# Two pairs of PSUM banks for the attention's output, rows normalised one unit later, expert 0's first chunk in the scores' banks

## The chip, the core and the metric

One core of one Trainium2 chip. The engines are TensorE (PE, with its weight loads as PEld), VectorE (DVE), ScalarE (ACT), GpSimd (POOL) and SyncE (SP, which here only issues transfers). Each runs its own instructions in order; semaphores tie them together. [...] The metric is the time of one execution on the device in microseconds, median of several runs.

## What is computed

Sliding-window attention over 8 batches of 8 heads, 576 positions, head dimension 64, then a mixture of 8 experts with two chosen per token, all in fp32:

```python
scores = scale * q @ k.T                       # masked to 0 <= pos_q - pos_k < 64
attn = exp(scores - max); attn /= sum(attn) + 1e-9
x = (attn @ v) as rows [4608, 512]             # token rows, heads side by side
noisy = x @ w_gate + log1p(exp(x @ w_noise)) * noise
top2 of noisy, softmax over the two -> weights
out = sum over the two chosen e of weight * (relu(x @ w1[e]) @ w2[e])
```

## The kernel before

**Units.** The attention runs over 36 units `j`: block `i` of 64 positions (nine) times a pair of batches `bp` (four). One unit gives 128 token rows. A unit needs four loads (`qc`, `KW`, `vt`, 256 KB each; `vw`, 272 KB) and one store of its rows to the DRAM tensor `X` (256 KB), all issued by SP. Since the window is one block long, a unit reads the keys and values of its own block and of the one before.

**The loop** (L723 on) is software-pipelined; the order of the calls in its body is the order of every engine's queue. In iteration `j` stand, in order: loads for units `j+2` and `j+3`; `scores(j)` (L242, TensorE, two banks `ps_s`); `soft_b(j-1)` (exp on ScalarE), `soft_a(j)` (ScalarE copies the scores), `pv(j-2)` (L300, 64 matmuls into the two banks `ps_o`, one pair); `soft_max(j)` (VectorE, masked copy), `norm_a(j-2)` (L318, VectorE: reciprocal of the row sums, and `gm`, the logits' share of `ps_o` times the reciprocal), `soft_max2(j)` (VectorE maximum, GpSimd subtraction); `norm_b(j-2)` (L327, ScalarE: eight copies of 64 elements with a per-row scale, `ps_o` to the tile `x`); `store(j-3)`; `transp(j-1)` (L283, TensorE, bank `ps_t`); `logits(j+1)` (L216, TensorE, bank `ps_x`, 16 matmuls of `vt` with the gate weights, whose result `logits_copy` (L226) puts beside the values so that `pv` carries the logits along); `apply_mask(j-1)` (VectorE, `ps_t` to `pt`); `gate(j-2)` (L342, VectorE sums `gm` over the heads).

**The routing** of 6 to 9 units (`route`, L396) is a list of small steps on `[128, n, 8]`, mostly on VectorE, some on ScalarE, with one rank computation on TensorE in bank `ps_g`. `drain(rate(q))` puts 0 to 2 of them at five places of each iteration, by `RATE` (L43); `HOLD` (L42) makes it skip some calls ahead of the rank matmul. Its results are scattered as list entries to DRAM by GpSimd, two transfers a unit of the routing, issued by `drain_slots`. GpSimd then gathers expert 0's rows by such a list, which SP loads.

**Expert 0's first chunk** (384 rows) starts inside the loop: `turn(0, 0)` (L575) transposes three gathered tiles on TensorE into the single bank `ps_m` and splits them in two parts on ScalarE and VectorE; it is set into iterations 31 and 32 (`TURN`, L36). `ahead` (L702) then places 15 of 32 steps of `up(0, 0)` (three matmuls each, accumulated in `ps_m`, four steps a tile) into iterations 33 to 36. After the loop the attention's banks are given to the experts, which run 24 chunks with TensorE at the centre.

**Banks before:** `ps_g` (warm-up, ranks), `ps_x` (logits), `ps_m` (expert 0's start), `ps_s` two, `ps_t` one, `ps_o` two: eight. `load_rest` (L169) issues in iteration 3 eight transfers: the noise, a zeroed stretch of `X`, and the padding of the lists.

Of the kernel before, what the change touches and what calls it, by code (L numbers as in the profile page):

```python
# [34 lines left out]
W1G = 12  # L35
TURN = 31  # L36
AHEAD = 15
SLOTS = 5
WARM = 4

ZEROS = (15, 28, 37)
HOLD = 4  # L42
RATE = ((15, 6), (20, 8), (26, 6), (99, 8))  # L43

# [19 lines left out]
def tile_kernel(ctx, tc, qT, kT, vx, vT, wgx, noise, w1, w2, out):  # L64
# [103 lines left out]

    def load_rest():  # L169
        nc.sync.dma_start(noise_sb, noise)  # L170
        nc.sync.dma_start(X[0:DUMP, :], zero)
        o = LIST * 2
        for n in CHUNKS:
            w = n // 32 * 2
            nc.sync.dma_start(rows(L, o, [[w, 32], [LIST * 2, E - 1], [1, w]]),
                              pad_f[:, None, :w].to_broadcast([32, E - 1, w]))
            o += n * 2
        pad_t = pad_o.rearrange("k p c -> k (p c)")
        nc.sync.dma_start(rows(L, 0, [[256, CAP // 128], [1, 256]]), pad_t[:CAP // 128])
        nc.sync.dma_start(rows(L, CAP // 128 * 256, [[256, 1], [1, CAP % 128 * 2]]), pad_t[:1, :CAP % 128 * 2])  # L180
        nc.sync.dma_start(rows(L, CAP * 2, [[256, OVT], [LIST * 2, E], [1, 256]]),
                          pad_o.rearrange("k p c -> k (p c)")[:, None, :].to_broadcast([OVT, E, 256]))

# [29 lines left out]

    VG = ps.tile([128, 4, 128], F32, name="ps_x")

    def logits(j):  # L216
        p = VG[:, j % 4]
        x = VT.pop(j)
        for u in range(2):
            for g in range(2):  # L220
                for a in range(2):
                    q = u * 2 + g
                    nc.tensor.matmul(p[a * 64:a * 64 + 64, q * 32:q * 32 + 32], lhsT=x[:, q, a * 64:a * 64 + 64],
                                     rhs=wgx_sb[:, g * 2 + a, :], start=True, stop=True)

    def logits_copy(j):  # L226
        i, bp = divmod(j, NP)
        nc.scalar.activation(VW[bp][:, i % 2, 4, :, :, 0:16].rearrange("p u k e -> p (u k) e"),
                             VG[:, j % 4].rearrange("p (k e) -> p k e", e=16), AF.Copy)

# [65 lines left out]

    PO, RS, GM = {}, {}, {}


    def pv(j):  # L300
        i, bp = divmod(j, NP)
        o = aps.tile([128, 2, 512], F32, name="ps_o")
        PO[j] = o[:, :, 0:340].rearrange("p a (k d) -> p a k d", d=85)
# [14 lines left out]
    def norm_a(j):  # L318
        r = wk.tile([128, 2, 4], F32, name="r")
        RS[j] = r  # L320
        nc.vector.tensor_scalar(r, PO[j][:, :, :, 16], 1e-9, None, op0=OP.add)
        nc.vector.reciprocal(r, r)
        GM[j] = wk.tile([128, 8, 16], F32, name="gm")
        nc.vector.tensor_tensor(GM[j].rearrange("p (a k) e -> p a k e", a=2), PO[j][:, :, :, 68:84],  # L324
                                r[:, :, :, None].to_broadcast([128, 2, 4, 16]), op=OP.mult)

    def norm_b(j, a):  # L327
        if j not in XT:
            XT[j] = gw.tile([128, H, 64], F32, name="x", bufs=3)
        o, r = PO[j][:, a, :, 0:68].rearrange("p k (q d) -> p k q d", d=17), RS[j][:, a]  # L330
        for k in range(4):
            nc.scalar.activation(XT[j][:, a * 4 + k].rearrange("p (q d) -> p q d", d=16), o[:, k, :, 0:16], AF.Copy,  # L332
                                 scale=r[:, k:k + 1])

    def store(j):
        nc.sync.dma_start(X[DUMP + j * 128:DUMP + (j + 1) * 128, :], XT.pop(j).rearrange("p h d -> p (h d)"))

# [237 lines left out]
    def turn(e, c):  # L575
# [6 lines left out]
        def f(q, m):  # L582
# [5 lines left out]
            else:  # L588
                y = bank()[:, :KD * m].rearrange("p (k m) -> p k m", k=KD)
                for k in range(KD):  # L590
# [7 lines left out]
        return [lambda q=q, m=m, x=x: x(q, m) for q, m in tiles(c) for x in (f, g)]  # L598

    def bank():  # L600
        if "up" in BANKS:
            return BANKS["up"].tile([128, 512], F32, name="ps_u", bufs=3)
        return ps.tile([128, 512], F32, name="ps_m")

# [115 lines left out]

    logits(0)
    logits_copy(0)
    for j in range(NT + 2):  # L723
        if j == TURN:
            for q, f in enumerate(turn(0, 0)):
                aux.setdefault(j + q // 3, []).append(f)
        if 0 < j < NT - 3:
# [10 lines left out]
        if NT - 2 <= j:  # L738
# [24 lines left out]
        on(gate, j - 2)  # L763
        drain(rate(3))
# [4 lines left out]
    store(NT - 1)  # L769
    for q in range(max(aux), NT + 1, -1):  # L770
        for f in aux.get(q, ()):
            f()
# [56 lines left out]
    ov = ctx.enter_context(tc.tile_pool(name="ov", bufs=1))  # L829

    def overflow(e, k):
        a1 = ov.tile([128, KD, F], F32, name="a1")
# [5 lines left out]
        if e == 0:  # L838
# [53 lines left out]
def layout(inputs):  # L892
# [44 lines left out]
```

## Time and profile before

| | |
|---|---|
| median of 3 runs | 1097.46 us (1096.47 to 1099.86) |
| the profiled execution | 1103.63 us, of it the span 1101.9 us |
| TensorE busy | 1015.8 us (92%) |
| VectorE, ScalarE, GpSimd busy | 454.0, 384.4, 537.7 us |
| transferred | 133.45 MB |

The profile's page and its queries are views of one execution, whose times count from the start of its span. "Busy" is the union of an engine's instructions; a matmul's end is modelled, so starts are the surer numbers. [...] A bracket at a row's end is the idle time of that engine just before, and what ended it; "issue" means nothing that the profile shows.

### The profile page before, as it was taken

What the parts mean: (1) busy time and instruction counts of PE and PEld (TensorE: products, weight loads), DVE (VectorE), ACT (ScalarE), POOL (GpSimd) and SP (SyncE); (2) the same over time, 40 slices, a digit from 0 to 9 for tenths busy, and PEclk for the clock granted to TensorE, in tenths of its full rate; (3) what the DMA queues carried; (4) which work ended last, traced back from release to release, by engine and by line L of the source; (5) the groups of instructions that cost most, each with busy time, mean ns of one, the idle gap of its engine ahead of it and who ended that gap; (6) DMA issues with size and microseconds to landing.
All of it is one profiled execution on the core that took longest, in us unless ns stands there. A gap on an engine that the chain in (4) does not pass through costs nothing. (4 is left out here: it accounts for less than half of the span.)

```text
span 1101.9 us, 20457 instructions
## 1 busy us (share of the span) xinstructions
PE 1015.8 (92%) x8313; PEld 902.1 (82%) x8313; DVE 454.0 (41%) x979; ACT 384.4 (35%) x975; POOL 537.7 (49%) x612
## 2 busy tenths in 40 slices
PE   8677776889996999999999999999999999999994
PEld 8566665778795889988998899888989888988893
DVE  5588676553134233522452244224422533262220
ACT  3566454432133223422342234224322522252220
POOL 4346544566255555453555356524654465455411
PEclk9899887999998999999999999999999999999997
DMA  8989977469824422632263235324423452333122
GB/s 290 342 253 253 234 187 263 127 178 229 230 55 129 103 48 51 202 55 39 45 204 57 40 92 157 58 37 121 130 49 44 115 134 46 51 51 53 37 25 31
DMA packets 62681, 133.45 MB, mean 121 GB/s; under 512 B 16776, under 2 KB 17266, under 8 KB 60786
## 3 DMA queue, kind: packets, MB, share of 16 engines
q1 hardware_dynamic: 39986, 92.11, 26.6%
q0 software_dynamic: 22592, 39.95, 20.7%
q8 instruction: 67, 1.10, 0.4%
q14 instruction: 36, 0.29, 0.1%
HBM read 92.31 MB, written 39.70 MB: 120 GB/s over the span
## 5 line engine op out<-in xcount | busy, mean ns | idle before, releaser
L570 POOL DMA_INDIRECT xg<-xrows,ixs x266 | 259.0, 974 | 81.2 <-issue 75.1
L626 PE MATMUL ps_u<-xh,w1h 128*128 128x384 f32 (+1 forms) x752 | 261.0, 347 | 12.1 <-ACT xh L596 11.4
L627 PE MATMUL ps_u<-xl,w1h 128*128 128x384 f32 (+1 forms) x752 | 260.8, 347 | 0.0
L628 PE MATMUL ps_u<-xh,w1l 128*128 128x384 f32 (+1 forms) x752 | 260.5, 346 | 0.0
L641 POOL DMA_INDIRECT out_dram<-yo,lts x70 | 113.1, 1615 | 295.8 <-ACT yo L661 152.5
L656 PE MATMUL ps_d<-w2h,hh 128*128 128x512 f32 x576 | 225.4, 391 | 0.0
L657 PE MATMUL ps_d<-w2l,hh 128*128 128x512 f32 x576 | 225.1, 391 | 0.0
L658 PE MATMUL ps_d<-w2h,hl 128*128 128x512 f32 x576 | 225.0, 391 | 0.0
L633 DVE SCALAR_TENSOR_TENSOR hl<-ps_u,hh 128x384 fp32r<-128x384 f32 x188 | 104.7, 557 | 269.6 <-ACT hh L632 269.6
L632 ACT ACTIVATE hh<-ps_u 128x384 fp32r<-128x384 f32 x188 | 92.5, 492 | 239.3 <-PE ps_u L628 239.1
L626 PEld LDWEIGHTS ps_u<-xh,w1h 128*128 128x128 f32 x752 | 142.1, 189 | 17.9 <-ACT xh L596 12.3
L627 PEld LDWEIGHTS ps_u<-xl,w1h 128*128 128x128 f32 x752 | 142.0, 189 | 5.5 <-DVE xl L597 0.9
L628 PEld LDWEIGHTS ps_u<-xh,w1l 128*128 128x128 f32 x752 | 142.0, 189 | 3.8
L656 PEld LDWEIGHTS ps_d<-w2h,hh 128*128 128x128 f32 x576 | 108.5, 188 | 23.7 <-issue 1.8
L658 PEld LDWEIGHTS ps_d<-w2h,hl 128*128 128x128 f32 x576 | 108.5, 188 | 22.8
L657 PEld LDWEIGHTS ps_d<-w2l,hh 128*128 128x128 f32 x576 | 108.5, 188 | 21.9
L661 ACT ACTIVATE yo<-ps_d,lts 128x512 f32<-128x512 f32 x63 | 43.4, 690 | 195.7 <-PE ps_d L658 118.4
L597 DVE TENSOR_TENSOR xl<-xy,xh 128x512 fp32r<-128x512 f32 (+1 forms) x70 | 46.7, 667 | 147.5 <-ACT xh L596 147.5
L332 ACT ACTIVATE x<-ps_o,r 128x64 f32<-128x64 f32 x288 | 63.2, 330 | 70.4 <-DVE gm L324 22.5
L276 POOL TENSOR_TENSOR t<-t,mx 128x512 f32<-128x512 f32 x36 | 37.5, 1042 | 99.4 <-DVE mx L275 47.9
L311 PE MATMUL ps_o<-vw,pt 64*64 64x85 f32 x2176 | 56.1, 254 | 24.7 <-ACT x L332 18.5
L472 POOL DMA_INDIRECT slots<-val,posi x72 | 70.6, 980 | 15.0 <-issue 14.5
(146 smaller groups left out, 964.7 us busy)
## 6 DMA issues: line engine op xcount, KB each, us to landing
w2s<-in_w_dram SPq DMA_DIRECT2D x7, 2048.0 KB
w1s<-in_w_dram SPq DMA_DIRECT2D x7, 2048.0 KB
vw<-in_vx_dram SPq DMA_DIRECT2D x36, 272.0 KB
out_dram<-zero SPq DMA_DIRECT2D x37, 256.0 KB
qc<-in_qT_dram SPq DMA_DIRECT2D x36, 256.0 KB
KW<-in_kT_dram SPq DMA_DIRECT2D x36, 256.0 KB
vt<-in_vT_dram SPq DMA_DIRECT2D x36, 256.0 KB
xrows<-x SPq DMA_DIRECT2D x36, 256.0 KB
```

The lines of the kernel that those rows point to most:

```text
L332: nc.scalar.activation(XT[j][:, a * 4 + k].rearrange("p (q d) -> p q d", d=16), o[:, k, :, 0:16], AF.Copy, scale=r[:, k:k + 1])
L472: s = nc.gpsimd.indirect_dma_start(out=L, out_offset=bass.IndirectOffsetOnAxis(ap=posi[:, c2, q:q + 1], axis=0), in_=val[:, c2, q, :], in_ ...
L570: nc.gpsimd.indirect_dma_start(out=XG[e, c, t // 4][:, t % 4, :], out_offset=None, in_=XQ[:(DUMP + seen.get((e, c), NT) * 128) * 4], in_of ...
L626: nc.tensor.matmul(p[:, :n], lhsT=w1h[:, k, fs], rhs=xh[:, k, :n], start=(k == 0), stop=False)
L627: nc.tensor.matmul(p[:, :n], lhsT=w1h[:, k, fs], rhs=xl[:, k, :n], start=False, stop=False)
L628: nc.tensor.matmul(p[:, :n], lhsT=w1l[:, k, fs], rhs=xh[:, k, :n], start=False, stop=(k == KD - 1))
L632: nc.scalar.activation(h, p[:, :main], AF.Relu)
L633: nc.vector.scalar_tensor_tensor(l, p[:, :main], 0.0, h.bitcast(F32), op0=OP.max, op1=OP.subtract)
L641: nc.gpsimd.indirect_dma_start(out=out[:DUMP + seen.get((e, c), NT) * 128], out_offset=bass.IndirectOffsetOnAxis(ap=LT[e, c][:m, q, 0:1], ...
L656: nc.tensor.matmul(p, lhsT=hh[f][:, sl], rhs=w2h[:, f, :], start=(f == 0), stop=False)
L657: nc.tensor.matmul(p, lhsT=hh[f][:, sl], rhs=w2l[:, f, :], start=False, stop=False)
L658: nc.tensor.matmul(p, lhsT=hl[f][:, sl], rhs=w2h[:, f, :], start=False, stop=(f == KF - 1))
```

## The change

`ps_o` becomes two pairs of banks. `norm_a`, `norm_b`, `store` and `gate` run one iteration later, so the loop has one iteration more; `norm_a` comes first in the iteration, `store` among the loads. `gm` is gone: `norm_b` copies 80 columns a head, the logits among them, to a tile whose order is part, head, column; `X` and `w1` take that order of columns, `w1` on the host. The logits' accumulators move from `ps_x` to the warm-up's bank, two slots for four, and `logits(j)` runs in iteration `j`. The routing's steps are drained at other places, `HOLD` is 6, `RATE` shifts by an iteration. `load_rest`'s transfers are spread over iterations 3 to 7. `turn(0, 0)` begins in iteration 33 at two steps an iteration, in the bank `ps_t`; 16 steps of `up(0, 0)` are placed in iterations 36 to 38, in the two banks of `ps_s` in turn. `ps_x` and `ps_m` are gone; the overflow code, which runs only where an expert has more rows than its list, gets a pool of its own.

```diff
-TURN = 31
-AHEAD = 15
+TURN = 33
+AHEAD = 16
...
-HOLD = 4
-RATE = ((15, 6), (20, 8), (26, 6), (99, 8))
+HOLD = 6
+RATE = ((16, 6), (21, 8), (27, 6), (99, 8))
...
+    REST = [lambda: nc.sync.dma_start(noise_sb, noise), lambda: nc.sync.dma_start(X[0:DUMP, :], zero),
+            lambda: load_pads(0), lambda: load_pads(1), lambda: load_pads(2)]
...
-    VG = ps.tile([128, 4, 128], F32, name="ps_x")
+    VG = idle[:, 0:256].rearrange("p (n c) -> p n c", n=2)
...
-        o = aps.tile([128, 2, 512], F32, name="ps_o")
+        o = aps.tile([128, 2, 512], F32, name="ps_o", bufs=2)
...
         nc.vector.reciprocal(r, r)
-        GM[j] = wk.tile([128, 8, 16], F32, name="gm")
-        nc.vector.tensor_tensor(GM[j].rearrange("p (a k) e -> p a k e", a=2), PO[j][:, :, :, 68:84],
-                                r[:, :, :, None].to_broadcast([128, 2, 4, 16]), op=OP.mult)
...
-            XT[j] = gw.tile([128, H, 64], F32, name="x", bufs=3)
-        o, r = PO[j][:, a, :, 0:68].rearrange("p k (q d) -> p k q d", d=17), RS[j][:, a]
+            XT[j] = gw.tile([128, 5, H, 16], F32, name="x", bufs=3)
+        o, r = PO[j][:, a].rearrange("p k (q d) -> p k q d", d=17), RS[j][:, a]
         for k in range(4):
-            nc.scalar.activation(XT[j][:, a * 4 + k].rearrange("p (q d) -> p q d", d=16), o[:, k, :, 0:16], AF.Copy,
-                                 scale=r[:, k:k + 1])
+            nc.scalar.activation(XT[j][:, :, a * 4 + k], o[:, k, :, 0:16], AF.Copy, scale=r[:, k:k + 1])
...
-        nc.vector.tensor_reduce(LG[c][:, j - ROUTE[c]], GM.pop(j).rearrange("p k e -> p e k"), op=OP.add, axis=AX.X)
+        nc.vector.tensor_reduce(LG[c][:, j - ROUTE[c]], XT[j][:, 4].rearrange("p h e -> p e h"), op=OP.add, axis=AX.X)
...
+        if not pair:
+            p = aps.tile([128, 2, 4, 128], F32, name="ps_s").rearrange("p u g c -> p u (g c)")
+            pair.extend([p[:, 1], p[:, 0]])
+        return pair.pop()
...
+        return aps.tile([128, 4, 128], F32, name="ps_t").rearrange("p k c -> p (k c)")
...
-            if j >= TURN + 2 and len(taken) < AHEAD:
+            if j >= NT and len(taken) < AHEAD:
...
-    logits(0)
-    logits_copy(0)
-    for j in range(NT + 2):
+    for j in range(NT + 3):
         if j == TURN:
             for q, f in enumerate(turn(0, 0)):
-                aux.setdefault(j + q // 3, []).append(f)
+                aux.setdefault(j + q // 2, []).append(f)
...
-        if j == 3:
-            load_rest()
+        on(store, j - 4)
+        if 2 < j < 3 + len(REST):
+            REST[j - 3]()
...
+        on(norm_a, j - 3)
+        drain(rate(0))
         on(scores, j)
         on(soft_b, j - 1)
         on(soft_a, j)
-        drain(rate(0))
-        ahead(1)
+        ahead(2)
+        drain(rate(1))
         on(pv, j - 2)
-        drain(rate(1))
+        on(norm_b, j - 3, 0)
         on(soft_max, j)
-        on(norm_a, j - 2)
         on(soft_max2, j)
         drain_slots(1)
-        on(norm_b, j - 2, 0)
-        on(store, j - 3)
-        drain(rate(2))
         if j < NP:
             warm(WARM)
-        ahead(1)
         on(transp, j - 1)
-        on(norm_b, j - 2, 1)
-        on(logits, j + 1)
         ahead(2)
+        on(logits, j)
+        on(norm_b, j - 3, 1)
         on(apply_mask, j - 1)
-        on(logits_copy, j + 1)
-        on(gate, j - 2)
+        drain(rate(2))
+        on(logits_copy, j)
+        ahead(2)
+        on(gate, j - 3)
```

## Rows read from the trace of the kernel before

**Rows 1.** By stretch: us, busy (x count) per engine, PEclk, DMA share, GB/s.

```profile
7.60:24.00 16.40, 16.31 (x302) 14.67 (x304) 8.21 (x17) 4.95 (x19) 4.59 (x7) 1.00 1.01 351
24.00:221.00 197.00, 147.48 (x3847) 125.55 (x3847) 137.62 (x371) 109.70 (x413) 95.63 (x143) 0.90 0.80 235
...
330.00:1101.90 771.90, 745.40 (x3661) 669.20 (x3659) 266.83 (x482) 236.38 (x470) 374.44 (x337) 0.99 0.35 79
```

**Rows 2.** Waits of PE, 0 to 221 us: total us, times, longest us.

```profile
PE ps_o L311 <- ACT x L332: 18.5, 18, 1.4
PE ps_x L223 <- DMA vt<-in_vT_dram: 9.3, 3, 4.1
PE ps_s L252 <- issue: 5.5, 3, 2.5
PE ps_o L311 <- issue: 5.4, 6, 3.1
```

**Rows 3.** Timeline of PE: start us, length us; scores of units 0, 9, 18, 33; expert 0.

```profile
8.58 1.13 PE L254 MATMUL ps_s<-KW,qc 64*64 64x64 f32 x32
...
51.05 1.10 PE L252 MATMUL ps_s<-KW,qc 64*64 64x128 f32 x32
...
97.05 1.10 PE L252 MATMUL ps_s<-KW,qc 64*64 64x128 f32 x32
...
193.07 1.99 PE L252 MATMUL ps_s<-KW,qc 64*64 64x128 f32 x32
...
221.78 0.34 PE L626 MATMUL ps_u<-xh,w1h 128*128 128x384 f32 x1
```

**Rows 4.** Timeline of all engines inside one unit, 95 to 100 us.

```profile
95.12 0.22 DVE L423 TENSOR_TENSOR l<-l,noise_sb 128x56 f32<-128x56 f32 x1
...
96.27 0.72 DVE L270 COPY_PREDICATED t<-mprev,ps_s 128x512 f32<-128x512 uint32 x1
...
97.31 0.29 DVE L324 TENSOR_TENSOR gm<-ps_o,r 128x128 f32<-128x128 f32 x1
...
97.68 1.75 ACT L332 ACTIVATE x<-ps_o,r 128x64 f32<-128x64 f32 x8 [2.09 <-PE ps_x L223]
...
98.22 1.22 DVE L293 TENSOR_TENSOR pt<-ps_t,maskT 128x1024 f32<-128x1024 f32 x1
...
99.36 0.36 DVE L346 TENSOR_REDUCE lg<-gm 128x16 f32<-128x128 f32 x1
...
99.54 1.28 PE L311 MATMUL ps_o<-vw,pt 64*64 64x85 f32 x57 [1.39 <-ACT x L332]
```

**Rows 5.** Timeline of PE: three long waits of the attention.

```profile
35.12 1.07 PE L223 MATMUL ps_x<-wgx_sb,vt 128*64 128x32 f32 x16 [4.06 <-DMA vt<-in_vT_dram]
...
168.40 1.07 PE L223 MATMUL ps_x<-wgx_sb,vt 128*64 128x32 f32 x16 [3.45 <-DMA vt<-in_vT_dram]
...
182.64 1.12 PE L591 MATMUL ps_m<-ident,xg 128*128 128x128 f32 x4 [3.09 <-DVE xl L597]
```

**Rows 6.** By stretch, single units; columns as in rows 1.

```profile
118.00:126.90 8.90, 6.45 (x120) 5.69 (x119) 5.47 (x17) 4.02 (x16) 3.44 (x6) 0.62 0.81 200
46.00:51.00 5.00, 3.66 (x116) 3.15 (x116) 3.23 (x7) 3.53 (x13) 2.47 (x3) 1.00 1.05 386
61.90:67.10 5.20, 3.70 (x119) 3.11 (x119) 4.97 (x14) 3.53 (x13) 2.47 (x3) 1.00 0.84 257
97.00:103.20 6.20, 3.96 (x124) 3.29 (x121) 5.73 (x19) 3.20 (x13) 4.16 (x7) 1.00 0.97 248
```

**Rows 7.** Timeline of PE: the step after the one at 221.78.

```profile
222.31 0.33 PE L626 MATMUL ps_u<-xh,w1h 128*128 128x384 f32 x1
```

**Rows 8.** The page: instruction queue's packets, MB; the scatters' group, idle before them.

```profile
q8 instruction: 67, 1.10, 0.4%
...
L472 POOL DMA_INDIRECT slots<-val,posi x72 | 70.6, 980 | 15.0 <-issue 14.5
```

**Rows 9.** Waits of PE, 221 to 450 us.

```profile
PE ps_u L591 <- DMA xg<-xrows,lt: 2.4, 1, 2.4
```

More of the change, by code (lines that the diff above doesn't have):

```diff
@@ L167, in tile_kernel, with load_pads @@
     noise_sb = consts.tile([128, NT, E], F32)
[L169 to L177, printed above, removed]
-        pad_t = pad_o.rearrange("k p c -> k (p c)")
[L179 to L182, printed above, removed]
+    def load_pads(q):
+        if q == 0:
+            o = LIST * 2
+            for n in CHUNKS:
+                w = n // 32 * 2
+                nc.sync.dma_start(rows(L, o, [[w, 32], [LIST * 2, E - 1], [1, w]]),
+                                  pad_f[:, None, :w].to_broadcast([32, E - 1, w]))
+                o += n * 2
+            return
+        pad_t = pad_o.rearrange("k p c -> k (p c)")
+        if q == 1:
+            nc.sync.dma_start(rows(L, 0, [[256, CAP // 128], [1, 256]]), pad_t[:CAP // 128])
+            nc.sync.dma_start(rows(L, CAP // 128 * 256, [[256, 1], [1, CAP % 128 * 2]]), pad_t[:1, :CAP % 128 * 2])
+        else:
+            nc.sync.dma_start(rows(L, CAP * 2, [[256, OVT], [LIST * 2, E], [1, 256]]),
+                              pad_t[:, None, :].to_broadcast([OVT, E, 256]))
+    REST = [lambda: nc.sync.dma_start(noise_sb, noise), lambda: nc.sync.dma_start(X[0:DUMP, :], zero),
+            lambda: load_pads(0), lambda: load_pads(1), lambda: load_pads(2)]
     def zero_out(t):
@@ L211, in split_w2 @@
         return [lambda f=f: split(w2s[:, f], W2["h"][:, f], W2["l"][:, f]) for f in range(KF)]
-    VG = ps.tile([128, 4, 128], F32, name="ps_x")
+    VG = idle[:, 0:256].rearrange("p (n c) -> p n c", n=2)
     def logits(j):
-        p = VG[:, j % 4]
+        p = VG[:, j % 2]
         x = VT.pop(j)
@@ L228, in logits_copy @@
         nc.scalar.activation(VW[bp][:, i % 2, 4, :, :, 0:16].rearrange("p u k e -> p (u k) e"),
-                             VG[:, j % 4].rearrange("p (k e) -> p k e", e=16), AF.Copy)
+                             VG[:, j % 2].rearrange("p (k e) -> p k e", e=16), AF.Copy)
     ST, T, P, TP, PT, XT = {}, {}, {}, {}, {}, {}
@@ L295, in apply_mask @@
                                 op=OP.mult)
-    PO, RS, GM = {}, {}, {}
+    PO, RS = {}, {}
     def pv(j):
         i, bp = divmod(j, NP)
-        o = aps.tile([128, 2, 512], F32, name="ps_o")
+        o = aps.tile([128, 2, 512], F32, name="ps_o", bufs=2)
         PO[j] = o[:, :, 0:340].rearrange("p a (k d) -> p a k d", d=85)
@@ L322, in norm_a @@
         nc.vector.reciprocal(r, r)
-        GM[j] = wk.tile([128, 8, 16], F32, name="gm")
-        nc.vector.tensor_tensor(GM[j].rearrange("p (a k) e -> p a k e", a=2), PO[j][:, :, :, 68:84],
-                                r[:, :, :, None].to_broadcast([128, 2, 4, 16]), op=OP.mult)
     def norm_b(j, a):
         if j not in XT:
-            XT[j] = gw.tile([128, H, 64], F32, name="x", bufs=3)
-        o, r = PO[j][:, a, :, 0:68].rearrange("p k (q d) -> p k q d", d=17), RS[j][:, a]
+            XT[j] = gw.tile([128, 5, H, 16], F32, name="x", bufs=3)
+        o, r = PO[j][:, a].rearrange("p k (q d) -> p k q d", d=17), RS[j][:, a]
         for k in range(4):
-            nc.scalar.activation(XT[j][:, a * 4 + k].rearrange("p (q d) -> p q d", d=16), o[:, k, :, 0:16], AF.Copy,
-                                 scale=r[:, k:k + 1])
+            nc.scalar.activation(XT[j][:, :, a * 4 + k], o[:, k, :, 0:16], AF.Copy, scale=r[:, k:k + 1])
     def store(j):
-        nc.sync.dma_start(X[DUMP + j * 128:DUMP + (j + 1) * 128, :], XT.pop(j).rearrange("p h d -> p (h d)"))
+        nc.sync.dma_start(X[DUMP + j * 128:DUMP + (j + 1) * 128, :],
+                          XT.pop(j)[:, 0:4].rearrange("p q h d -> p (q h d)"))
     LG, PG = {}, {}
@@ L588, in f @@
             else:
-                y = bank()[:, :KD * m].rearrange("p (k m) -> p k m", k=KD)
+                y = turn_bank()[:, :KD * m].rearrange("p (k m) -> p k m", k=KD)
                 for k in range(KD):
@@ L598, in turn @@
         return [lambda q=q, m=m, x=x: x(q, m) for q, m in tiles(c) for x in (f, g)]
+    pair = []
     def bank():
@@ L602, in bank, with turn_bank @@
             return BANKS["up"].tile([128, 512], F32, name="ps_u", bufs=3)
-        return ps.tile([128, 512], F32, name="ps_m")
+        if not pair:
+            p = aps.tile([128, 2, 4, 128], F32, name="ps_s").rearrange("p u g c -> p u (g c)")
+            pair.extend([p[:, 1], p[:, 0]])
+        return pair.pop()
+    def turn_bank():
+        if "up" in BANKS:
+            return bank()
+        return aps.tile([128, 4, 128], F32, name="ps_t").rearrange("p k c -> p (k c)")
     EXB, BANKS = {}, {}
@@ L737, in tile_kernel @@
             load_w1(0, slice(k, k + 1))
-        if NT - 2 <= j:
+        if NT - 2 <= j < NT + 2:
             load_w2(0, slice((j - NT + 2) * 2, (j - NT + 3) * 2))
+        on(norm_a, j - 3)
+        drain(rate(0))
         on(scores, j)
@@ L769, in tile_kernel @@
     store(NT - 1)
-    for q in range(max(aux), NT + 1, -1):
+    for q in range(max(aux), NT + 2, -1):
         for f in aux.get(q, ()):
@@ L829, in tile_kernel @@
     ov = ctx.enter_context(tc.tile_pool(name="ov", bufs=1))
+    ops = ctx.enter_context(tc.tile_pool(name="ops", bufs=1, space=bass.MemoryType.PSUM))
     def overflow(e, k):
@@ L842, in overflow @@
                                          in_offset=bass.IndirectOffsetOnAxis(ap=lt[:, 0:1], axis=0))
-            xp = ps.tile([128, KD, 128], F32, name="ps_x")
+            xp = ops.tile([128, KD, 128], F32, name="ps_x")
             for d in range(KD):
@@ L865, in overflow @@
         for f in range(KF):
-            hp = ps.tile([128, 128], F32, name=("ps_m", "ps_x")[f % 2])
+            hp = ops.tile([128, 128], F32, name=("ps_m", "ps_x")[f % 2])
             for d in range(KD):
@@ L912, in layout @@
     noise = inputs["moe_noise"].reshape(NP, 2, NB, 64, E).transpose(1, 3, 2, 0, 4).reshape(128, NT, E)
-    w1 = inputs["moe_w1"].reshape(E, 4, KD, 32, F).transpose(0, 1, 3, 2, 4).reshape(E, 128, KD, F)
-    w1 = np.concatenate([inputs["moe_w1"][:1].reshape(1, KD, 128, F).transpose(0, 2, 1, 3), w1[1:]])
+    w1x = inputs["moe_w1"].reshape(E, H, 4, 16, F).transpose(0, 2, 1, 3, 4).reshape(E, DM, F)
+    w1 = w1x.reshape(E, 4, KD, 32, F).transpose(0, 1, 3, 2, 4).reshape(E, 128, KD, F)
+    w1 = np.concatenate([w1x[:1].reshape(1, KD, 128, F).transpose(0, 2, 1, 3), w1[1:]])
     w2 = inputs["moe_w2"].reshape(E, KF, 128, DM).transpose(0, 2, 1, 3)
```

## The prediction

> **What bounds the kernel now.** I read the view by stretch first. From 330 us to the end TensorE is busy 745 of 772 us: the experts are bound by it and the change doesn't touch them. From 24 to 221 us it is busy 147 of 197, at a granted clock of 0.90 [rows 1]. So whatever is won is won in the attention, some 215 us, and the rest is carried along. The waits of TensorE in that stage say what ends last [rows 2]: `pv` (L311) waits for `norm_b` (L332) 18 times, 18.5 us in all; `logits` (L223) for its load 9.3 us; and 10.9 us at L252 and L311 have no releaser ("issue"). One more wait of 3.1 us belongs to expert 0's transposes and the bank they share [rows 5].
>
> The starts of `scores` (L254, L252) cut the stage [rows 3]: units 0 to 8 take 42.5 us (8.58 to 51.05), 9 to 17 take 46.0 (to 97.05), 18 to 32 take 96.0 (to 193.07), and 28.7 more go by until expert 0's first chunk runs alone (221.78). An undisturbed unit takes 46.0 / 9 = 5.1 us.
>
> Inside one unit [rows 4] the order is a loop: `pv` must end before the reciprocal, `norm_b` takes 1.75 us behind it, and the next `pv` starts only when `norm_b` is through (99.54, after a wait of 1.39), since there is one pair of output banks. VectorE is nearly full in the same unit: from the copy at 96.27 to the gate at 99.36 are 3.1 us without a hole, the gate takes 0.3, and each drained step of the routing 0.22, 0.25 with the gap behind it.
>
> **The change part by part.**
>
> *Two pairs of banks, rows normalised one unit later.* `pv(j-2)` then waits for `norm_b(j-4)`, done a whole unit earlier: the 18.5 us leave the loop. What is late next? TensorE's own work is 3.7 us a unit (3.70 busy of 5.20 [rows 6]). VectorE's is the 3.1 + 0.3 above, less `gm` (L324, 0.29 busy, some 0.25 with the overlap at its ends), so 3.15, and the routing. Four routings of 32 VectorE steps each fall on units 9 to 35, 0 to 8 a unit by the drain's rates: 0 to 2.0 us. A unit costs the larger of 3.8 (TensorE and a semaphore or so) and 3.1 + 0.24 n. With n read off the drain's lists unit by unit, the sums are 38.7 us for units 9 to 17 and 66.1 for 18 to 32, about 4.35 a unit.
>
> *Logits with the rows.* `gm` goes. `norm_b` writes 80 elements for 64, eight times a unit. The eight take 1.75 us [rows 4]; were all of that per element it would grow by 0.44, and not at all if it were fixed; I take 0.2. ScalarE is busy 3.53 of 5.20 us [rows 6], so either end is hidden. `gate` now reads what ScalarE writes, and everything of VectorE stands behind it. I place `norm_b`'s end 2.8 us after `scores` ends (copy 0.85, eight rows 1.95) and the gate's turn 3.3 after it (copy 0.7, maximum 0.7, mask 1.2, one routing step, semaphores). The margin is 0.5 us, so zero; if the cover is gone each unit pays what ScalarE is late beyond it.
>
> *Logits' matmuls one unit closer to their use, in the warm-up's bank.* A load of `vt` is waited for by `logits(j)` at the end of unit j and no longer by unit j-1's end. Its issue moves behind `logits(j-1)` on SP, because the three buffers come free later; from issue to use I count 12.3 us (three units of 4.35 less 0.7) against 10.6 (two units of 5.1 and 0.4), 1.7 us more lead. The two long waits (35.12 and 168.40, 4.06 and 3.45 us [rows 5]) follow, in SP's order, the eight transfers of `load_rest` and expert 0's list, which waits for the scatters. The first is cut into five units. Behind the second, a `vt` issued in unit 30 is now wanted at the end of unit 31 or later. I count both as gone. The warm-up bank costs nothing: TensorE writes it in order, VectorE reads its routing part once per routing.
>
> *`load_rest` spread, `store` a unit later.* The same eight transfers pass SP in units 3 to 7 and not in unit 3; `store(j-4)` waits for a `norm_b` long done, where it stood behind the list and the copy. By the tiles a unit moves 4 x 256 + 272 KB = 1.33 MB; at 4.35 us that is 305 GB/s. The DMA engines moved 386 in one unit, and 257 at a share of 0.84 in a usual one [rows 6], so it fits with little room. In units 0 to 8 it binds: some 14.6 MB by the tiles are issued before unit 9's operands, at the 351 GB/s of the start [rows 1] 42 us. With scores ahead of logits in unit 0, which need not wait for `vt` (0 to 2.8 us; 2 taken), unit 9 starts at about 45, not 51: 6 us saved (3 to 8).
>
> *Expert 0's first transposes in units 33 to 35, one tile each, in the transposes' bank.* Units 31 and 32 hold the 3.09 us wait [rows 5] and one like it, with the low clock after them; that is in the 96.0. The new place costs VectorE a pass of 0.7, TensorE four transposes of about 0.7 together, and up to 0.7 of waiting for `apply_mask`, a unit: 5.3 us for each of three units, 15.9 in all.
>
> *The head start of expert 0 (16 steps) after the last scores.* A step is 0.53 us (221.78 to 222.31 [rows 7]). In units 36 to 38 TensorE then has 16 x 0.53 + 2 x 1.4 + 0.7 = 12 us, with 2 us before the first step for the third tile's split (an estimate: two passes over 128x512 on ScalarE and VectorE, each like the copy's 0.72 [rows 4], and semaphores) and 1 us of ends: 15. So from unit 33 on 30.9 us stand against 28.7: 2 lost (3 won to 8 lost).
>
> *Units 18 to 32.* To the 66.1 come the "issue" waits. [...] They come while the DMA engines are full; instructions come by DMA too (67 packets [rows 8]), so I read them as late code. Nothing in the change takes them away. I leave 10 us: 76 against 96, 20 saved (8 to 28).
>
> *Units 9 to 17:* 46.0 - 38.7 = 7.3 saved (2.7 to 9).
>
> *HOLD and the rates* move the routing's steps by a unit. Two scatters more are left when the loop ends, 1.19 us each on POOL's queue ((70.6 + 15.0) / 72 [rows 8]) ahead of the gathers, while TensorE already waits 2.4 us for a gather of expert 0's third chunk [rows 9]: 1 us lost (0 to 3).
>
> The overflow code's banks move and it isn't run; `w1`'s new order is made on the host.
>
> **Sum.** 6 + 7.3 + 20 - 2 - 1 = 30 us. The profiled execution takes 1103.6 us (span 1101.9), 6.2 above the median 1097.5. So 1073.5 for a profiled run and 1067.5 for the median: **1068 us**.
>
> **The rivals.**
>
> *VectorE is the new loop.* The unit in [rows 4] has no hole in VectorE, and is 5.0 us long with 8 routing steps. If routing steps that wait for ScalarE and the gate's margin cost 0.4 us a unit more than I allow, units 9 to 35 keep 4.75: 27 x 0.4 = 11 us less, 1079. Against it: between routings it has 2 us to spare.
>
> *The transfers bind.* One unit shows a share of 0.97 at 248 GB/s [rows 6], while the routing's scatters run; if that is a ceiling, a unit can't fall below 1.33 MB / 248 = 5.35 us, units 9 to 28 win nothing and only the start, the two loads and the transposes do: 6 + 9 + 3 - 3, about 1083 to 1088. Against it: 386 GB/s in another unit.
>
> *Late code goes away.* The waits depend on where the fetch falls against a burst of loads; with other phases they could fade, 10 us and more: 1053 to 1058. [...]
>
> [...]
>
> *It doesn't do what it says.* If `pv` still waits on ScalarE (ScalarE in order behind the copy of the scores), the units stay at 5 us and the later tail eats the rest: 1094 to 1100.
>
> **How the numbers follow.** Forecast (1060 to 1077) 0.48; VectorE (1077 to 1083) 0.17; transfers (1083 to 1090) 0.09; late code gone (1048 to 1060) 0.14; no effect 0.05; slower 0.07. Range 1052 to 1088, which takes in most of the first four. A measurement here tells 0.3% (3.3 us) from no change: faster 0.88, same 0.05, slower 0.07.
>
> **What would show it.** Right: the wait of L311 for L332 falls from 18.5 to under 3 us; undisturbed units of 4.3 us, 3.8 where nothing is drained; L223 waits under 2 us for its loads; scores of unit 9 near 45 us; the clock over the stage at 0.95; expert 0 alone near 192 us. Wrong: VectorE's gate waiting for L332 in most units; "issue" waits in more than 16 units; units of 5 us with a DMA share near 1; a longer wait than 6 us for the third chunk's gather.

## The result, and the profile after

The kernel after takes 1082.0 us (median of four runs, 1080.3 to 1083.0) against 1097.3 for the kernel before (four runs, 1096.5 to 1099.9): ratio 0.9855, 95% interval 0.9833 to 0.9878. It is faster by 15.3 us (1.45%), where 29.5 were forecast. The profiled execution of after took 1081.1 us, with a span of 1079.3 and a granted clock (PEclk in the rows: what TensorE was granted, as a share of full speed; the traces of before and after hold the values 0.50 and 1.00 alone, so one between them is a mean) of 0.979; before it was 1103.6, 1101.9 and 0.968. Between the two profiled executions lie 22.5 us.

The same cuts as in [rows 3], from the timeline of TensorE in after (start, duration, engine, line, operation, count, and in brackets the idle time and what ended it):

```profile
5.69 0.54 PE L259 MATMUL ps_s<-KW,qc 64*64 64x64 f32 x12
...
40.89 0.34 PE L257 MATMUL ps_s<-KW,qc 64*64 64x128 f32 x4
...
89.30 0.34 PE L257 MATMUL ps_s<-KW,qc 64*64 64x128 f32 x4
...
169.14 0.32 PE L257 MATMUL ps_s<-KW,qc 64*64 64x128 f32 x1
...
204.36 0.44 PE L640 MATMUL ps_u<-xh,w1h 128*128 128x384 f32 x1 [1.17 <-DVE hl L647]
```

These are the scores of units 0, 9, 18 and 33, and the first step of expert 0 that runs alone. The lengths between them, against those of before and against the forecast:

| stretch | before, us | after, us | gain | gain forecast |
|---|---|---|---|---|
| start to unit 9 | 51.05 | 40.89 | 10.2 | 6 |
| units 9 to 17 | 46.0 | 48.4 | -2.4 | 7.3 |
| units 18 to 32 | 96.0 | 79.8 | 16.2 | 20 |
| unit 33 to expert 0 alone | 28.7 | 35.2 | -6.5 | -2 |
| from there to the end | 880.1 | 874.9 | 5.2 | -1 |
| sum | | | 22.7 | 30 |

Waits of TensorE in after up to 204 us (tile, line, what was waited for: us in all, times, longest), to be held against [rows 2]:

```profile
PE ps_o L316 <- issue: 20.2, 13, 3.5
PE ps_s L257 <- issue: 9.3, 7, 2.1
PE ps_g L228 <- issue: 3.6, 3, 2.2
PE ps_t L594 <- DVE pt L298: 3.0, 3, 1.1
PE ps_s L640 <- DVE hl L647: 2.3, 2, 1.2
```

The wait of `pv` for `norm_b` (18.5 us in 18 waits before) is not there any more. What stands in its place has no releaser: 33.6 us in 24 waits, where before had 16.9 in 12 up to 222 us (10.9 of them at the two lines of [rows 2]). The waits for loads, 9.3 us before, are down to 0.2.

Busy time, granted clock, share of the DMA engines and GB/s by stretch in after (columns as in [rows 1]); the second is units 9 to 15 alone:

```profile
24.00:204.00 180.00, 137.04 (x3709) 118.18 (x3702) 126.10 (x334) 114.78 (x411) 97.51 (x149) 0.94 0.87 254
40.90:75.60 34.70, 26.52 (x819) 22.75 (x817) 29.22 (x67) 26.91 (x97) 16.38 (x20) 1.00 0.99 352
330.00:1079.00 749.00, 733.27 (x3609) 658.64 (x3607) 258.04 (x469) 228.86 (x457) 359.79 (x325) 0.99 0.35 78
```

In units 9 to 15 the DMA engines have no room: a share of 0.99 at 352 GB/s. One unit of that stretch:

```profile
57.36 0.47 PE L316 MATMUL ps_o<-vw,pt 64*64 64x85 f32 x13
58.81 0.20 DVE L327 RECIPROCAL r<-r 128x8 f32<-128x8 f32 x1
59.05 1.85 ACT L335 ACTIVATE x<-ps_o,r 128x80 f32<-128x80 f32 x8 [0.60 <-DVE r L327]
59.24 1.24 PE L316 MATMUL ps_o<-vw,pt 64*64 64x85 f32 x51 [1.42 <-issue]
61.59 1.10 PE L257 MATMUL ps_s<-KW,qc 64*64 64x128 f32 x32
62.51 0.40 PE L316 MATMUL ps_o<-vw,pt 64*64 64x85 f32 x12
```

The scores are done, `pv` begins at 57.36, and after 13 of its 64 multiplications TensorE stands still for 1.42 us with all operands ready: VectorE's reciprocal for the other unit is done at 59.01 and ScalarE writes rows from 59.05 on. The unit takes 5.15 us from `pv` to `pv`, no less than in before (5.1).

What such a wait is can be read by counting. I numbered TensorE's instructions of the trace (16806 in after: 16626 weight loads and multiplications, and 180 of its sequencer, most of them waits for semaphores) from 0 and took each step of over 0.45 us from one start to the next that ended at a number 193 above a multiple of 256, up to 175 us:

```
after   21 steps, 37.0 us    before   9 steps, 15.9 us
some of after: ends at  42.73   48.53   53.93   59.24   64.61   81.24  134.97  154.40
               length    1.45    2.04    1.41    1.65    1.72    3.76    3.50    3.50
```

In both kernels every wait without a releaser of over 0.4 us between unit 9 and unit 33 ends at such a number, but for two of 0.8 ahead of `pv` in after (94.58 and 99.55, each 0.10 us after VectorE's `pt` is done) and one of 2.84 ahead of expert 0's transposes in before (192.05). TensorE's code comes on queue 8 in 67 packets [rows 8], 16.4 KB each; 16806 / 256 is 65.6. Around the wait above the DMA queues hold one of them (window 56.4 to 58; queue, kind: packets, MB, share of 16 engines):

```profile
q1 hardware_dynamic: 321, 0.59, 100.2%
q8 instruction: 1, 0.02, 3.7%
```

That packet runs from 56.9 to 57.9, and TensorE goes on 1.36 us after its end. Over all waits this last step is 1.0 to 1.6 us with few exceptions. So a wait is code that comes late, in blocks of 256 instructions. In units 9 to 15 six such packets start, 2.7 us in the mean (1.0 to 3.5) after the present block began to run (2.7 in before too); a packet takes 1.0 and is followed by 1.35: 5.1 us a block. A unit is 235 instructions, so 4.7 us of code. The next packet, of the block that begins at 73.24, starts 5.0 us into it, and the longest wait stands behind it (81.24). By these means the change from block to block is hidden in units 9 to 15 of after only where 256 instructions take some 5.1 us or more.

In ten of the twelve experiments every kernel was slower from about 85 us on (before itself in 1167 to 1190 us), so I read those by their ratio to before beside them, and in detail only from the start to unit 18.

### The profile page after: what moved, and what is told of

The parts are those of the page before. It is cut to its first block, busy times and chain, and to the rows that moved or that the text cites. A ratio compares the mean times of both kernels' runs of the same rounds, so it can differ in the third digit from the quotient of the medians.

```text
span 1079.3 us, 20457 instructions
## 1 busy us (share of the span) xinstructions
PE 1004.2 (93%) x8313; PEld 894.3 (83%) x8313; DVE 444.0 (41%) x943; ACT 391.4 (36%) x975; POOL 534.3 (50%) x612
## 5 line engine op out<-in xcount | busy, mean ns | idle before, releaser
L640 PE MATMUL ps_u<-xh,w1h 128*128 128x384 f32 (+1 forms) x752 | 260.7, 347 | 11.5 <-ACT xh L599 10.3
L281 POOL TENSOR_TENSOR t<-t,mx 128x512 f32<-128x512 f32 x36 | 37.5, 1042 | 78.0 <-DVE mx L280 74.5
L316 PEld LDWEIGHTS ps_o<-vw,pt 64*64 64x64 f32 x2176 | 51.3, 143 | 25.4 <-issue 23.9
```

Source lines behind the costliest of these rows:

```text
L316: nc.tensor.matmul(PO[j][u * 64:u * 64 + 64, a, g * 2 + x, :], lhsT=pt[pa, w, u * 2 + g, x * 64:x * 64 + 64], rhs=v[pa, (i + w) % 2, :, u, ...
L640: nc.tensor.matmul(p[:, :n], lhsT=w1h[:, k, fs], rhs=xh[:, k, :n], start=(k == 0), stop=False)
```

## The experiments

The theory was that late code took the place of the removed wait and that loads make it late. The rivals were that VectorE's chain sets the unit, and that the second pair was not what won. "Units 9 to 15" below is the time from unit 9's scores to unit 16's: 36.3 us in before, 34.7 in after.

**Fewer bytes in after.**

```diff
     def load_qk(j):
+        if j >= 8:
+            QC[j] = QK[j % 4]
+            return
         i, bp = divmod(j, NP)
-        QC[j] = ld.tile([128, H, 64], F32, name="qc", bufs=4)
+        QC[j] = QK[j % 4] = ld.tile([128, H, 64], F32, name="qc", bufs=4)
```

> The kernel after, but from unit 8 on no q and no k is loaded (the four tiles already there are used again): 512 KB of the 1.33 MB of a unit go, and the scores from unit 8 on are computed from the wrong rows; the instructions of all engines but SP's loads stay. Late code (instructions of TensorE come by DMA on queue 8 and are late under load): the waits without a releaser fall from 33.6 us before expert 0 runs alone to under 12, units 9 to 32, 128.3 us now (5.34 each), come to 4.4 to 4.6 each, 106 to 110 us, and the time falls by 16 to 26 us, to 1056 to 1066. VectorE is the loop: the instructions and their order are the same, so units stay at 5.2 to 5.4 and the time within 3 us of 1082; what had no releaser turns into waits for VectorE or ScalarE.

Measured: ratio to before 0.9875 (0.9811 to 0.9939). The fall of 16 to 26 us against after did not come; after itself stands at 0.9855 and, measured again, at 0.9904, so the whole time decides nothing. But units 9 to 15 take 32.6 us, 4.66 each, where after has 34.7, and unit 18 starts at 82.6 (89.3). `pv` in four units, ScalarE and VectorE ahead of the second of them, and the stretch by engine (columns as above):

```profile
53.08 1.69 PE L319 MATMUL ps_o<-vw,pt 64*64 64x85 f32 x64 [0.79 <-ACT w1h L211]
57.73 1.40 PE L319 MATMUL ps_o<-vw,pt 64*64 64x85 f32 x64 [0.74 <-ACT w1h L211]
62.37 1.41 PE L319 MATMUL ps_o<-vw,pt 64*64 64x85 f32 x64 [0.79 <-ACT w1h L211]
67.02 1.41 PE L319 MATMUL ps_o<-vw,pt 64*64 64x85 f32 x64 [0.79 <-ACT w1h L211]
...
56.41 1.22 DVE L301 TENSOR_TENSOR pt<-ps_t,maskT 128x1024 f32<-128x1024 f32 x1
...
56.99 0.47 ACT L211 ACTIVATE w1h<-w1s 128x256 fp32r<-128x256 f32 x1
...
42.20:74.80 32.60, 26.31 (x818) 22.23 (x814) 28.61 (x67) 26.48 (x97) 16.02 (x20) 1.00 0.69 200
```

All 64 multiplications run through, 4.65 us from unit to unit; what is left to wait for, 0.8 us, is ahead of `pv`. The profile puts it down to ScalarE, but that is done at 57.46; VectorE's `pt` is done at 57.63, and in each of the four units `pv` starts 0.10 us after it. VectorE has no hole in these units. A packet of code now starts 1.6 us after the present block began, and only two of the waits at block ends are left (2.0 us; 8.3 in after). So the loads make the code late, as expected. And behind it VectorE's loop stands where the prediction put it: 3.15 + 6 x 0.24 = 4.59 us for a unit with six routing steps, 4.65 measured. The rival, unchanged units, is out for this stretch.

**Fewer bytes in before.** The same edit.

> The same cut of 512 KB a unit from unit 8 on (no q, no k; wrong scores) in the kernel before. Late code: its 15.3 us of waits without a releaser fall under 5 and the load waits of the logits (9.3 us) go, but pv still waits for norm_b, so undisturbed units stay at 5.0 to 5.1 us: 1082 to 1090, a fall of 8 to 15. Against the kernel after with the same cut the change is then worth 20 to 30 us and not 15. If the loads have nothing to do with the waits: 1094 to 1098.

Measured: ratio 0.9972 (0.9926 to 1.0018). Units 9 to 15 take 36.25 us, against 36.31 with all loads, at 159 GB/s instead of 271. The waits of TensorE there, first with fewer bytes, then in the kernel before:

```profile
PE ps_o L314 <- ACT x L335: 8.1, 6, 1.4
```

```profile
PE ps_o L311 <- ACT x L332: 8.6, 7, 1.4
PE ps_s L252 <- issue: 0.5, 1, 0.5
```

112 GB/s less change nothing: before the change `pv` waited for other engines and the code came meanwhile. The forecast of units of 5.0 to 5.1 held (5.18); that of 8 to 15 us for the whole time did not, nor that the change would be worth 20 to 30 us with light loads (0.9875 against 0.9972 is about 1%); why stays open. In units 9 to 15 the change is worth 3.7 us with light loads and 1.6 with all.

The profile names ScalarE's `norm_b` alone, but two engines end that wait together. In [rows 4] `pv` starts at 99.54; the rows are done at 99.43, and VectorE's `pt`, which `pv` reads, at 99.44. In the kernel before, each `pv` of units 7 to 17 starts 0.10 to 0.16 us after its `pt` and 0.05 to 0.12 us after the rows of the unit before it, and VectorE's waits in units 9 to 15 come to only 3.5 of 36.3 us (3.2 of 32.6 in after with fewer bytes). So VectorE's queue set before's unit as much as `norm_b` did. Of the 3.7 us, 3.4 are work that VectorE no longer has in these units: seven `gm` at 0.25 us, and seven routing steps at 0.24, which are drained later now (23 here where before has 30; 56 from unit 33 on where before has 45). No run takes `gm` away alone.

**One pair, and two pairs without the unit later.** Both take the reciprocal, the rows and the gate back to unit j-2; the store stays where after has it. The first also takes the second pair away.

```diff
-        o = aps.tile([128, 2, 512], F32, name="ps_o", bufs=2)
+        o = aps.tile([128, 2, 512], F32, name="ps_o")       # one_pair alone
...
-        on(norm_a, j - 3)
         drain(rate(0))
...
-        on(norm_b, j - 3, 0)
         on(soft_max, j)
+        on(norm_a, j - 2)
         on(soft_max2, j)
         drain_slots(1)
+        on(norm_b, j - 2, 0)
...
-        on(norm_b, j - 3, 1)
+        on(norm_b, j - 2, 1)
...
-        on(gate, j - 3)
+        on(gate, j - 2)
```

> The kernel after with one pair of output banks, and reciprocal, rows, store and gate back at unit j-2 behind pv, as before the change; everything else of the change stays (logits from the rows, loads spread, expert 0's places). If the second pair is worth the waits that it removed: pv waits for norm_b for 15 to 20 us again and the time rises by 15 to 25, to 1097 to 1107. Late code: most of the fetches hide behind that wait again, so the waits without a releaser fall to about 15 us, the two nearly cancel in the loop, and the time rises by only 5 to 12, to 1087 to 1094.

> The kernel after with its two pairs of banks, but reciprocal, rows, store and gate at unit j-2 behind pv, as before the change. The gate then reads rows that ScalarE writes in the same unit. If the unit later matters: VectorE's gate waits for norm_b 0.5 to 1 us in most units, units grow by as much, and the time rises by 10 to 25 us, to 1092 to 1107. If late code sets the unit (5.16 us where 0.4 to 1 of it is spare), the waits hide in it: within 5 us of 1082.

Measured: 1.008 (1.0037 to 1.0123) and 1.0066 (1.0025 to 1.0108) of before: both slower than before, and 1.6 to 2.3% behind after (0.9855 and, again, 0.9904). Units 9 to 15 take 39.2 and 40.6 us, at a granted clock of 0.87 and 0.96 where after and before have 1.00. The waits there, TensorE's in the first, then TensorE's and VectorE's in the second:

```profile
PE ps_o L316 <- ACT x L335: 5.4, 4, 2.2
PE ps_g L455 <- ACT vw L233: 2.4, 1, 2.4
```

```profile
PE ps_o L316 <- DVE pt L298: 4.3, 5, 0.9
```

```profile
DVE t L275 <- ACT t L267: 4.0, 3, 1.7
DVE lg L349 <- ACT x L335: 3.4, 6, 2.3
```

With one pair the wait for `norm_b` is back, now the last to end (`pv` starts 0.05 us after the rows, 0.3 or more after `pt`). With two pairs and the old time it is not, but `pv` waits for VectorE's `pt` in its place, and VectorE's gate waits for the rows (3.4 us in 6 waits; none in after), so the units are no shorter. The second pair without the later rows is worth nothing: it is the two together. The rise of 15 to 25 and of 10 to 25 us that I had given to the plain mechanism fits both (2.3% of 1082 are 24); what I had given to late code, 5 to 12 and within 5, fits neither.

**Units of 256 instructions.** Ten tiny multiplications, 20 instructions, are added to each unit; `pad(0)` adds none.

```diff
+    def pad(n):
+        for _ in range(n):
+            nc.tensor.matmul(idle[0:32, 500:501], lhsT=ones_b[:, 0:32], rhs=ones_b[:, 0:1], start=True, stop=True)
...
         on(logits, j)
+        if j == 8:
+            pad(0)
+        if 8 <= j < NT:
+            pad(10)
```

> The kernel after with ten tiny bf16 multiplications (into an unused column) behind the logits of each unit from 8 on, so that a unit is about 256 TensorE instructions and not 235; some 0.4 us of TensorE work a unit, all else as it is. Late code in blocks of 256 instructions: the wait in pv, which moves by about 11 multiplications from unit to unit in the trace of after, stands at the same place (within 2 multiplications a unit) in all undisturbed units, and its size is the same in each, between 0 and 2 us by where the block ends fall: 1065 to 1115, not within 3 us of after plus its share of the padding. VectorE's loop: TensorE has 0.6 us and more to spare in a unit, so the padding hides: within 4 us of 1082, and the waits without a releaser stay scattered over pv.

Measured: ratio 0.9992 (0.9964 to 1.002), 0.9 to 1.4% behind after. Scores of units 11 to 17, each from its wait on (unit 15 has none):

```profile
55.05 1.23 PE L257 MATMUL ps_s<-KW,qc 64*64 64x128 f32 x26 [1.15 <-issue]
61.02 0.98 PE L257 MATMUL ps_s<-KW,qc 64*64 64x128 f32 x26 [0.24 <-issue]
66.59 0.97 PE L257 MATMUL ps_s<-KW,qc 64*64 64x128 f32 x25 [1.42 <-issue]
72.14 1.15 PE L257 MATMUL ps_s<-KW,qc 64*64 64x128 f32 x25 [1.42 <-issue]
...
77.39 1.10 PE L257 MATMUL ps_s<-KW,qc 64*64 64x128 f32 x32
...
82.39 0.98 PE L257 MATMUL ps_s<-KW,qc 64*64 64x128 f32 x26 [0.28 <-issue]
88.61 0.98 PE L257 MATMUL ps_s<-KW,qc 64*64 64x128 f32 x26 [2.08 <-issue]
```

All waits without a releaser from 50 to 90 us are in the scores (6.6 us in 6), with 26 or 25 of 32 multiplications to go: the block ends have stopped wandering. In the count above, the number 193 falls on the 9th to 16th instruction of the scores (of 65) in every unit from 9 to 33. That is the block of 256, shown by moving it. Their size isn't the same, as I had expected, but 0 to 3 us, since the packet starts 2.3 to 4.8 us after its block began. Units 9 to 15 take 40.8 us, 5.8 each, where after has 5.0, with no more waiting at block ends (8.6 us against 8.3); why the padding costs so much is not shown.

**Expert 0's banks apart.**

```diff
         if not pair:
             p = aps.tile([128, 2, 4, 128], F32, name="ps_s").rearrange("p u g c -> p u (g c)")
-            pair.extend([p[:, 1], p[:, 0]])
-        return pair.pop()
+            pair.extend([p[:, 0], p[:, 1]])
+        pair.append(pair.pop(0))
+        return pair[-1]
```

> The kernel after, but expert 0's first 16 steps take the two halves of one pair of the scores' banks in turn, each free as soon as its own hl is through; as it is, the pair is handed out anew as a whole and waits for the hl of both halves. If the wait is that of the whole pair: the two waits of 1.17 us for hl (at 193.66 and 200.81 in the trace of after) fall under 0.2 and the time falls by 2 to 3.5 us against after, ratio to before 0.982 to 0.984. If ScalarE and VectorE behind them (hh and hl) are what is late: the waits move to the next bank, ratio 0.985 to 0.987 as for after.

Measured: ratio 0.9869 (0.9824 to 0.9915), no other than after. The head start, at the change from its first to its second bank:

```profile
234.52 0.52 PE L643 MATMUL ps_s<-xh,w1l 128*128 128x384 f32 x1
235.08 0.49 ACT L647 ACTIVATE hh<-ps_s 128x384 fp32r<-128x384 f32 x1 [25.02 <-PE ps_s L643]
235.60 0.56 DVE L648 SCALAR_TENSOR_TENSOR hl<-ps_s,hh 128x384 fp32r<-128x384 f32 x1 [24.30 <-ACT hh L647]
236.22 0.69 PE L641 MATMUL ps_s<-xh,w1h 128*128 128x384 f32 x1 [1.17 <-DVE hl L648]
```

The wait of 1.17 us is still there, and it is not what I took it for: the second half waits for the `hl` that reads the first half of the same pair. That two tiles for the halves would take it away was not tried.

**After again, and w1 later.** The kernel after once more; then with `w1` loaded in units 12 to 24; then with the banks of the last experiment as well.

```diff
-        if W1G - 8 <= 2 * j < W1G - 8 + 4 * KD and j % 2 == 0:
-            k = (j * 2 - W1G + 8) // 4
+        if W1G <= j < W1G + 4 * KD and j % 4 == 0:
+            k = (j - W1G) // 4
             load_w1(0, slice(k, k + 1))
...
-        aux.setdefault(W1G // 2 + q // 2, []).append(f)
+        aux.setdefault(W1G + 3 + q, []).append(f)
```

> The kernel after, unchanged, on the chip of the other kernels of this call, since the chips of the earlier experiments run the kernel before in 1185 to 1190 us and not in 1097. If what the change gains doesn't hang on that: ratio to before 0.983 to 0.988, as in its own measurement (0.9855). If the slower chips eat it: 0.992 to 1.0.

> The kernel after with expert 0's w1 loaded in units 12, 16, 20 and 24 (not 2, 4, 6 and 8) and split one piece a unit in units 15 to 30 (not two a unit in 6 to 13). Transfers bind the start, and their backlog is what makes the fetches late until unit 15: 2 MB of the 14.6 MB that stand ahead of unit 9 go, 5.7 us at 351 GB/s, so unit 9's scores start at 35 to 37 us and not 40.9; the waits at block ends before 85 us fall from 16 to under 8; half of it is lost again where the 2 MB now fall: 4 to 9 us faster than after. If bytes that are only moved win nothing, because the same fetches are late elsewhere: within 2 us of after.

> w1_later and banks_apart together. The two touch different stretches, so the gains add: 2 to 3 us faster than w1_later and 6 to 12 faster than after. If the head start of expert 0 waits for its later w1 or its splits instead: slower than w1_later.

Measured: 0.9904 (0.9861 to 0.9948), 0.9968 (0.9931 to 1.0005) and 0.9927 (0.9878 to 0.9977). After repeats its gain (1.0% here, 1.45% in its own measurement); 0.9904 falls between the two ranges that I had set, and the two intervals overlap. With `w1` later unit 8 starts at 33.9 and 33.7 us, against 37.5 and 38.2 in the two traces of after: the start is bound by bytes (a share of 1.00 at 352 GB/s from 7.6 to 40.9 us of after), and 2 MB are 4 us of it. It doesn't last: unit 9, expected at 35 to 37, starts at 41.3 and 37.9 (40.9 and 41.6 in after), and unit 18 at 86.6 and 86.8 (89.3 and 89.9; banks_apart, the same kernel up to there, 86.7), and the whole time is no better, also not with the banks. The waits at block ends up to 85 us, expected to fall from 16 us to under 8, are 14.6 and 13.9 (12.6 in after beside them). Bytes that are moved win nothing here, as the rival had it.

**Fewer bytes, again.** The first edit, beside after.

> As after_fewer (no q and no k loaded from unit 8 on, wrong scores from there), again, beside the kernel after itself. Late code: between units 8 and 17 the waits at block ends go (7.1 us before 85 us and none behind unit 8 in the first run), units are 4.6 us where VectorE has 6 routing steps. VectorE's loop alone: units of 5.2 as in after. Over the whole kernel late code expects 10 us and more against after on a chip that runs before in 1097; on a chip that runs it in 1185, where most of TensorE's waits behind 85 us stand at other places, 0 to 5.

Measured: 0.9909 (0.9872 to 0.9947), as after beside it. Units 9 to 15 take 32.4 us (35.4 in after_again), 4.63 each, with 1.3 us of waits at block ends (5.0). What the first run showed of this stretch is repeated; what fewer bytes would do to units 18 to 32 stays open.

**The two parts of the start.** The eight small transfers in unit 3 again, and the logits one unit earlier again. Before took 1094.7 us beside them.

```diff
-        if 2 < j < 3 + len(REST):
-            REST[j - 3]()
+        if j == 3:
+            for f in REST:
+                f()
```

```diff
+    logits(0)
+    logits_copy(0)
     for j in range(NT + 3):
...
-        on(logits, j)
+        on(logits, j + 1)
...
-        on(logits_copy, j)
+        on(logits_copy, j + 1)
```

> The kernel after with the eight small transfers (noise, the zero rows, the pads) all in unit 3 again, as before the change. Read at unit 9, where its scores start: 40.9 and 41.6 us in the two traces of after. If the change's spread is what took away the 4.06 us wait of the logits: that wait comes back, 3 to 4.5 us, and unit 9 starts at 44 to 46. If the bytes bind the start and not their order, or the logits' new place alone covers it: no load wait over 1 us and unit 9 at 40.5 to 42. Whole time: 0 to 4 us more than after.

> The kernel after with the logits and their copy one unit earlier again (unit 0's ahead of the loop, those of unit j+1 at the end of unit j), as before the change, in the two columns of the new bank. If the later place of the logits covers the loads of vt: the first scores start at 8 to 9 us and not 5.7, the logits wait for vt 4 to 9 us in the first 85 us (0.2 in after), and unit 9 starts at 43 to 46. If it covers nothing: the first scores 2 to 3 us later, but unit 9 within 1 us of 41, since the bytes ahead of it are the same.

Measured: 0.9825 (0.9785 to 0.9866) and 0.9891 (0.9857 to 0.9925); neither interval stands clear of after's. With the transfers in unit 3 the logits wait once more, 2.14 us (3 to 4.5 expected), and unit 9 starts at 42.6 (44 to 46 expected):

```profile
31.47 0.66 PE L228 MATMUL ps_g<-wgx_sb,vt 128*64 128x32 f32 x16 [2.14 <-DMA vt<-in_vT_dram]
```

So spreading them is worth 1 to 1.7 us at unit 9, and nothing that the end shows. With the logits early the first scores start at 8.87 and unit 9 at 49.21, later than I had expected (43 to 46):

```profile
7.87 1.07 PE L228 MATMUL ps_g<-wgx_sb,vt 128*64 128x32 f32 x16 [2.87 <-DMA vt<-in_vT_dram]
42.49 0.54 PE L228 MATMUL ps_g<-wgx_sb,vt 128*64 128x32 f32 x12 [2.05 <-issue]
48.96 0.31 PE L228 MATMUL ps_g<-wgx_sb,vt 128*64 128x32 f32 x1 [2.55 <-issue]
```

The load of `vt` is waited for once, in unit 0; the rest of the delay is at block ends, 8.1 us of waits before unit 9 (4.1 in after). But units 9 to 17 then take 41.1 us, and unit 18 starts at 90.27, 1 us behind after. The start's gain of 8 us is given back by unit 18.

No experiment gave a version that is clearly faster than after.

## Why the prediction was right, and where it was not

**What bounds the kernel, and that the wait would go:** right that it would go, half right on its cause. `pv`'s wait for `norm_b` is gone, and one_pair brings it back. But the prediction has the next `pv` start "only when `norm_b` is through", and in before VectorE's `pt` was done within 0.1 us of it; a second pair alone would have left `pv` waiting for `pt`, as in rows_same_unit (4.3 us in 5 waits). That VectorE had no hole in a unit of 5.0 us stands in the prediction, as a rival and not as a bound of before. The gate's margin of 0.5 us held (no wait in units 9 to 15; rows_same_unit shows the wait without it). Eight rows take 1.85 us, 0.1 more than before, where 0.2 was taken. The clock over the stage is 0.94, forecast 0.95.

**A unit of 3.15 + 0.24 n:** right as VectorE's loop, shown with fewer bytes (4.65 against 4.59). Wrong as the length of a unit in after: TensorE's code was missing from the list of what could be late next. The prediction knew of late code, but priced it only as a leftover of units 18 to 32 and as a rival. In units 9 to 17 before has 0.8 us of it and after 12.0; 38.7 us were forecast and 48.4 came.

**"It fits with little room", at 305 GB/s:** the step that let that through. The 1.33 MB of a unit leave out 2 MB of `w1` and the backlog of the start; 352 GB/s flowed at a share of 0.99. The rival in which transfers bind was right for units 0 to 15, and the sign named for it came, units of 5 us (4.96) with a share near 1; but by this rate and not by the 248 GB/s at which I priced it, and with late code as what TensorE feels of it, not a wait for operands.

**Units 0 to 8, 6 us:** 10.2 came, and they are not a term of their own. Start and units 9 to 17 draw on the same transfers: 28.4 MB by unit 18 in after (40.9 us at 330 GB/s and 48.4 at 308). With the full loads five runs of after or near it reach unit 18 at 86.7 to 90.3 us, whichever way the start went. The two terms should have been one, 97.05 to about 89: 7.8 won, not 13.3.

**Units 18 to 32, 20 us:** 16.2. Waits at block ends were left at 10 us, a size that no run shows: they are 19.0 us in 11 waits (15.1 in 8 before). That is the mis-sized term; what is left of the stage, 60.8 us, is less than the 66.1 of the sum, so 3.8 us of the 9 show. The sign that I had named, "issue" waits in more than 16 units, did come: 21 at block ends. It didn't decide: one costs 1.8 us in the mean (37.0 / 21), and before pays 15.9 for nine itself. After the wait that ended at 81.24, the longest, the granted clock from 80 to 90 us is 0.66 (0.50 from 81.5 to 87.5, 1.00 from 88 on).

**Unit 33 to expert 0 alone:** 35.2 us against 30.9. Units 33 to 35 take 18.5, not 15.9: the transposes wait 1.0 us each for the mask, where the whole bank change was put at up to 0.7, and one block end costs 1.6. The head start takes 16.7, not 15: three waits of 1.17 for `hl` were not foreseen. Expert 0 runs alone from 204.4 us on, not from near 192.

**After the loop:** 1 us lost was forecast, 5.2 were won. The gather is waited for 2.4 us as before [rows 9], so HOLD cost nothing. The rank's two waits fell from 3.0 to 1.0 us, those for `xh` from 11.4 to 10.3, and one more step was done; 2 us are not located.

**From the profiled run to the median:** 6.0 us were taken off (1073.5 to 1067.5) because the profiled execution of before was 6.2 above its median. That of after is 0.9 below its own. The sum missed the profiled time by 7.6 us (1073.5 against 1081.1); the other 6.9 of the miss are this step.

**How much of it was luck:** the five terms of the sum missed by +4.2, -9.7, -3.8, -4.5 and +6.2 us (plus is more won than forecast). That they leave only 7.6 us is luck. So is that 1082.0 lies in the band of a rival, VectorE as the new loop (1077 to 1083, at 0.17): what lengthened units 9 to 15 was late code, not 0.4 us a unit more of VectorE.

## What to carry to other kernels

When a wait leaves a loop, list what else was hidden behind it, the engine's own code among it: in units 9 to 15 of after a loop of small multiplications used up 256 instructions in 5.1 us, the time that a block of code needed to come. Count the instructions of a unit and hold their time against the start of the code's packets; a wait without a releaser that ends at the same number within 256 (here 193) is that. And terms that draw on the same full transfers are one term; what one wins early the other can lose (here 10.2 us by unit 9, of which 7.8 were left at unit 18). Where a wait is put down to one engine, look at what else its instruction reads and when that is done: with two chains that end together, taking one away won nothing here (rows_same_unit, 1.0066 of before).

## What the runs showed of the hardware

Late code has a price per block. Under the full loads of units 9 to 15 (352 GB/s) it is 2.7 us from the begin of a block to the packet of the next, 1.0 for the packet and 1.35 until TensorE goes on, so 5.1 us for 256 instructions. With the fewer bytes (192 to 200 GB/s) the first is 1.4 to 1.6 us and the packet 1.1; with the same last step that makes some 4 us, an estimate, since TensorE hardly waited there. In the experts, where a block lasts some 26 us, the packet mostly starts 19 to 35 us into it, not at its begin; what sets its start the traces don't show. And a wait for code holds up loads: around the longest one SP's load of `vw` waits 5.8 us for `pv`, and from 81.5 to 83 us the DMA engines move next to nothing (a share of 0.00).
